# Attention and two feed-forward layers on one core: split tiles written through ACT's queue, three raw buffers, whole weight tiles, a held attention chain with work on POOL

## The chip, the cores and the metric

One core of a Trainium2 chip runs the whole program. TensorE (PE) has 128 rows and columns; VectorE (DVE), ScalarE (ACT) and GpSimd (POOL) work on its results, and SyncE (SP) issues DMAs. The metric is device time in microseconds of one execution.

## The reference

The first layer is a linear attention over 8 batches of 8 heads, 576 positions and 64 columns; its output, 4608 tokens by 512, goes through a squared-ReLU feed-forward layer of width 2048, then through RMS normalisation and a gated layer of width 1536. All is float32; the weights come as float64.

```python
q_s = exp(q - max(q, -1));  q_s = q_s / (sum(q_s, -1) + 1e-09)
k_s = exp(k - max(k, 2));   k_s = k_s / (sum(k_s, 2) + 1e-09)
kv = einsum('bhsd,bhse->bhde', k_s, v)
x = einsum('bhsd,bhde->bhse', q_s, kv)        # then as 4608 x 512
r = maximum(x @ moe_w_in, 0.0);  x = (r * r) @ moe_w_out
xn = x / sqrt(mean(x * x, -1) + 1e-06) * rms_g
g = xn @ w_gate
out = (g * (1 / (1 + exp(-g))) * (xn @ w_val)) @ w_out
```

## The kernel before

The 4608 tokens are nine blocks of 512. Stage 1 does attention and the first feed-forward layer of all blocks, stage 2 the gated layer, with a Strassen-like scheme of seven products of halves (STEPS).

Every operand of PE is split into two reduced-precision parts, the rounded value (ACT, L73) and the remainder (DVE, L74), and each product is three passes of PE over those parts (mm3, L92).

A unit of stage 1 is one 128-column slice c of the 2048 columns for one block j: p1_A (L526) does 12 matmuls into ps_h, ReLU, square and split; p1_B (L538), two units later, 12 matmuls into the accumulators. There are 16 units a block and 144 in all. In between, each unit runs what is due at it: weight preparation (tick, L308) and attention of the next block (todo, L763).

Weight preparation takes a tile of 128 by 512 float64 words through four stages, one stage a tick: d_load (DMA into one of two raw buffers, by SP), d_words (POOL takes the high words, L211, and ACT the low ones, L219), d_float (three operations on DVE, L230 to L242) and d_split (the rounded copy on ACT, L246, and the remainder on POOL, L247). In block 0 the 32 tiles of the first layer are made, about two a unit, and used at once from a ring of seven; all but eight, which stay, are also written to DRAM, by a DMA on SP's queue right after the split (L253). In blocks 1 to 6 the tiles of the gated layer follow, with sums and differences of quarters on POOL (L278), and are written through two buffers so (L261 to L263), again by SP. Later blocks load split tiles from DRAM into the ring (feed, L159); SP waits at each load for the slot's last reader.

Attention works in pairs of heads, hp = 0 to 3, four for each block. A_STEPS (L760) gives each step's unit beside the pair's start, A_STARTS, every three units: k and q are loaded three units ahead (a_load), v one ahead, then come the maxima and the q-subtraction with its exponential (a_q), a unit later the normalisation of q (a_qn, L455) and the spreading of k's column maxima (a_ktr, with PE for blocks 0 and 1 and DVE transposes after), then q's transposes on PE (a_qT), the k-subtraction (L427) and exponential (a_kexp), a unit later the product of k and v and its normalisation into block-diagonal tiles kvd (a_kv, with L493 and L494), and a unit later the product with q (a_x) into ps_x and its split x, which is the operand of the next block's p1_A. q, k and v tiles have two buffers each.

The program is traced in this order, and a scheduler then orders each engine's instructions by its own cost model and tells each what to wait for; on the chip each engine runs its list in order. `tc.keep_in_program_order(ins)` pins an instruction behind everything already traced on its engine.

Of the kernel before, what the change touches and what calls it, by code (L numbers as in the profile page):

```python
# [24 lines left out]
def attention_moe_kernel(  # L25
# [7 lines left out]
    w_gate: bass.AP,  # L33
    w_val: bass.AP,
# [4 lines left out]
    nc = tc.nc  # L39
# [8 lines left out]
    FF1 = w_in.shape[1] // P  # L48
    FF2 = w_gate.shape[1] // P
# [19 lines left out]
    ]  # L69
    x2d = [tc.dram_tile([P, KD, T], F32, name=f"x2d{j}") for j in range(NB)]  # L70
# [31 lines left out]
    NTAG = 8  # L102
# [81 lines left out]

    raws, words, floats = {}, {}, {}

    def halves(n, c, r):
        rows = slice(r * (DM // 2), (r + 1) * (DM // 2))
        cols = slice((2 * n + c) * P, (2 * n + c + 1) * P)
        return [w[rows, cols].rearrange("(k p) f -> p k f", p=P) for w in (w_gate, w_val)]  # L190

    def d_load(key):
        n, c = key
        r = pools["d"].tile([P, 512], U64, tag="raw", name="raw", bufs=2)
        if n == "i":
            src = w_in[:, c * P : (c + 1) * P].rearrange("(k p) f -> p k f", p=P)
            nc.sync.dma_start(out=r.rearrange("p (k f) -> p k f", k=KD), in_=src)
        elif n in ("o", "u"):
            w = w_out if n == "o" else w_out2
            nc.sync.dma_start(out=r, in_=w[c * P : (c + 1) * P, :])  # L200
        else:
            for g, src in enumerate(halves(c, int(n[0]) - 1, int(n[1]) - 1)):
                rv = r.rearrange("p (g k f) -> p g k f", g=2, k=2)
                nc.sync.dma_start(out=rv[:, g], in_=src)
        raws[key] = r
# [102 lines left out]
    def tick():  # L308
        n = ticks[0]
        for stage, ahead in ((d_split, 0), (d_float, 1), (d_words, 2), (d_load, 3)):  # L310
            if 0 <= n - 3 + ahead < len(jobs):
                key = jobs[n - 3 + ahead]
                if key is None:
                    continue
                if stage == d_split and n - 3 + ahead >= NJ1:
                    stage = d_quad
                stage(key)
        ticks[0] += 1

# [4 lines left out]
    kts, kes, vts, qts, qns, mks, mcs, qTs = {}, {}, {}, {}, {}, {}, {}, {}  # L324
# [9 lines left out]
    def a_load(j, hp):  # L334
        hs = slice(2 * hp, 2 * hp + 2)
        if j < B:
            kt = a_tile(j, hp, [2, SF + 1, D], "kt")
            nc.gpsimd.memset(kt[SR:P, :, SF, :], -3e38)
            nc.sync.dma_start(
                out=kt[:, :, 0:SF, :],  # L340
                in_=k[j, hs, 0 : SF * P, :].rearrange("h (p c) d -> p h c d", c=SF),
            )
            nc.sync.dma_start(
                out=kt[0:SR, :, SF, :], in_=k[j, hs, SF * P : S, :].rearrange("h p d -> p h d")
            )
            kts[j, hp] = kt
        qt = a_tile(j, hp, [2, NG, D], "qt")
# [38 lines left out]
    def a_ktr(j, hp):  # L386
        if j >= B:
            return
        if j > 1:
# [3 lines left out]
            mb = pools["a"].tile([P, P], F32, tag="mb", name="mb", bufs=1)  # L393
# [19 lines left out]
        mb = pools["a"].tile([P, P], F32, tag="mb", name="mb", bufs=1)  # L413
# [3 lines left out]
    def a_kexp(j, hp):  # L417
# [7 lines left out]
        kt = kts.pop((j, hp))  # L425
        mx = ps[:, 0:P].rearrange("p (h d) -> p h d", h=2).unsqueeze(2)
        nc.vector.tensor_tensor(  # L427
            out=kt, in0=kt, in1=mx.to_broadcast([P, 2, SF + 1, D]), op=ALU.subtract
        )
        ke = pools["a"].tile([P, SF + 1, 2, D], F32, tag="ke", name="ke", bufs=1)  # L430
        nc.scalar.activation(out=ke, in_=kt.rearrange("p h c d -> p c h d"), func=AF.Exp)
        kes[j, hp] = ke

    def a_q(j, hp):
        qt = qts[j, hp]
        qv = qt.rearrange("p h c d -> p (h c) d")
        n = 2 * NG
        qm = pools["a"].tile([P, n], F32, tag="qm", name="qm")
        nc.vector.reduce_max(out=qm, in_=qv, axis=AX.X)
        (nc.gpsimd if j == 0 else nc.vector).tensor_tensor(  # L440
            out=qv, in0=qv, in1=qm.unsqueeze(2).to_broadcast([P, n, D]), op=ALU.subtract
        )
        nc.scalar.activation(out=qv, in_=qv, func=AF.Exp)

    def a_qn(j, hp):
        qt = qts.pop((j, hp))
        qv = qt.rearrange("p h c d -> p (h c) d")
        n = 2 * NG
        qs = pools["a"].tile([P, n], F32, tag="qs", name="qs")
        nc.vector.reduce_sum(out=qs, in_=qv, axis=AX.X)  # L450
        nc.vector.tensor_scalar_add(out=qs, in0=qs, scalar1=1e-9)
        nc.vector.reciprocal(out=qs, in_=qs)
        qn = pools["a"].tile([P, NG, 2, D], F32, tag="qn", name="qn", bufs=2)
        rs = qs.rearrange("p (h c) -> p h c", h=2).unsqueeze(3)
        nc.vector.tensor_tensor(  # L455
# [16 lines left out]
    def a_kv(j, hp):
# [4 lines left out]
        for c in range(SF + 1):  # L477
            m = P if c < SF else SR
            for h in range(2):
                nc.tensor.matmul(  # L480
# [5 lines left out]
                )  # L486
        rk = pools["a"].tile([P, 1], F32, tag="rk", name="rk")
        nc.vector.tensor_scalar_add(out=rk, in0=ps[:, D : D + 1], scalar1=1e-9)
        nc.vector.reciprocal(out=rk, in_=rk)
        t = kvd[j % 2][hp]  # L490
        for h in range(2):
            r = slice(h * D, (h + 1) * D)
            nc.vector.tensor_scalar_mul(out=t[r, 0, r], in0=ps[r, 0:D], scalar1=rk[r])  # L493
            nc.vector.scalar_tensor_tensor(  # L494
                out=t[r, 1, r],
                in0=ps[r, 0:D],
                scalar=rk[r],
                in1=t[r, 0, r].bitcast(F32),
                op0=ALU.mult,
                op1=ALU.subtract,  # L500
            )

    def a_x(j, hp):
# [5 lines left out]
        for b, lo, hi in ((j - 1, 0, p0), (j, p0, P)):  # L509
            if lo == hi:  # L510
# [266 lines left out]
    with ExitStack() as ctx_a:  # L777
# [5 lines left out]
        for hp in range(NP):  # L783
            a_load(0, hp)
# [6 lines left out]
        for row in kvd:  # L791
            for t in row:
                nc.gpsimd.memset(t.bitcast(F32), 0.0)
# [3 lines left out]
            "m": a_kmax, "q": a_q, "n": a_qn, "r": a_ktr, "e": a_kexp, "t": a_qT, "v": a_kv, "x": a_x  # L797
        }
        for step in (
# [5 lines left out]
            else:  # L805
                first[step[0]](0, int(step[1]))
# [6 lines left out]
        for i, (j, c) in enumerate(units):  # L813
# [60 lines left out]


# [27 lines left out]
```

## Time and profile before

| | |
|---|---|
| Median of 3 runs | 1823.58 us (1822.58 to 1827.39) |
| Profiled execution | 1824.28 us, its span 1822.5 us |
| PE, PEld busy | 1750.0 us (96%), 1516.4 us (83%) |
| DVE, ACT, POOL busy | 1163.1 us (64%), 744.9 us (41%), 227.3 us (12%) |
| DMA | 423.35 MB, mean 232 GB/s |

The page cuts the span into 40 slices of 45.6 us; a digit is the busy share in tenths:

```profile
PE   5888989999999999999999999999999999999998
...
DVE  8987987768687654321336666675767676757544
ACT  3654545555545434333443333423233333333322
POOL 4553224333414100000000000000000000000000
```

The first 21 digits are stage 1. POOL's work ends with weight preparation, in the 14th. A share averages over stages: what an engine costs is read where others wait for it.

### The profile page before, as it was taken

What the parts mean: (1) busy time and instruction counts of PE and PEld (TensorE: products, weight loads), DVE (VectorE), ACT (ScalarE), POOL (GpSimd) and SP (SyncE); (2) the same over time, 40 slices, a digit from 0 to 9 for tenths busy, and PEclk for the clock granted to TensorE, in tenths of its full rate; (3) what the DMA queues carried; (4) which work ended last, traced back from release to release, by engine and by line L of the source; (5) the groups of instructions that cost most, each with busy time, mean ns of one, the idle gap of its engine ahead of it and who ended that gap; (6) DMA issues with size and microseconds to landing.
All of it is one profiled execution on the core that took longest, in us unless ns stands there. A gap on an engine that the chain in (4) does not pass through costs nothing.

```text
span 1822.5 us, 27487 instructions
## 1 busy us (share of the span) xinstructions
PE 1750.0 (96%) x10298; PEld 1516.4 (83%) x10298; DVE 1163.1 (64%) x2080; ACT 744.9 (41%) x1279; POOL 227.3 (12%) x265
## 2 busy tenths in 40 slices
PE   5888989999999999999999999999999999999998
PEld 3666878778877888888888989898999999999997
DVE  8987987768687654321336666675767676757544
ACT  3654545555545434333443333423233333333322
POOL 4553224333414100000000000000000000000000
PEclk9998999999999999999999999999999999999999
DMA  6778878898878855445767666767676767676673
GB/s 191 228 235 267 269 249 290 268 298 268 299 259 286 267 177 172 160 140 208 256 214 233 221 246 215 242 222 255 209 257 213 255 209 261 212 244 217 214 237 131
DMA packets 190244, 423.35 MB, mean 232 GB/s; under 512 B 57888, under 2 KB 95776, under 8 KB 188960
## 3 DMA queue, kind: packets, MB, share of 16 engines
q1 hardware_dynamic: 190112, 421.60, 69.6%
q8 instruction: 82, 1.34, 0.3%
q14 instruction: 50, 0.41, 0.1%
HBM read 361.76 MB, written 59.77 MB: 231 GB/s over the span
## 4 chain that ended last, share of the span: by engine, by line
PE 76%; DVE 10%; DMA 6%; issue 2%; ACT 2%; SPq 2%; POOL 1%; DVEq 0%; POOLq 0%; ACTq 0%
PE acc L94 31%; PE ps_h L94 15%; PE ps_x L668 8%; PE ps_y L668 8%; PE ps_v L668 8%; PE ps_w L668 4%; DMA kt<-in_k_dram 2%; DMA out_dram<-e 2%; DVE t L242 1%; DVE t L238 1%; PE ps_x L94 1%; DVE g L74 1%; DVE t L230 1%; PE ps_kv L480 1%; DVE mk L381 1%
## 5 line engine op out<-in xcount | busy, mean ns | idle before, releaser
L94 PE MATMUL ps_h<-x,ws 128*128 128x512 f32 x1296 | 328.3, 402 | 5.7 <-POOL ws L247 4.7
L94 PE MATMUL acc<-g,ws 128*128 128x512 f32 x1296 | 315.5, 392 | 7.8 <-ACT ws L246 3.4
L74 DVE TENSOR_TENSOR g<-r,g 128x512 fp32r<-128x512 f32 x252 | 186.9, 742 | 172.6 <-ACT g L73 169.9
L94 PEld LDWEIGHTS acc<-g,ws 128*128 128x128 f32 x1296 | 243.3, 188 | 62.2 <-ACT ws L246 4.2
L94 PEld LDWEIGHTS ps_h<-x,ws 128*128 128x128 f32 x1296 | 242.8, 192 | 59.2 <-POOL ws L247 7.0
L94 PE MATMUL acc<-ws,g 128*128 128x512 f32 x1080 | 267.1, 392 | 0.0
L94 PEld LDWEIGHTS acc<-ws,g 128*128 128x128 f32 x1080 | 195.5, 189 | 36.4
L73 ACT ACTIVATE g<-r 128x512 fp32r<-128x512 f32 x252 | 157.9, 627 | 35.1 <-DVE r L652 30.8
L650 ACT ACTIVATE sg<-c 128x256 f32<-128x256 f32 x108 | 56.5, 523 | 262.8 <-DVE c L683 213.3
L532 ACT ACTIVATE r<-ps_h 128x512 f32<-128x512 f32 x144 | 85.3, 593 | 190.6 <-PE ps_h L94 190.0
L683 DVE TENSOR_TENSOR u<-ps_y,p 128x512 f32<-128x512 f32 x108 | 73.9, 684 | 124.2 <-PE ps_y L668 124.2
L668 PE MATMUL ps_x<-x,ws 128*128 128x256 f32 x972 | 130.5, 284 | 10.1 <-ACT p L699 10.1
L668 PEld LDWEIGHTS ps_x<-x,ws 128*128 128x128 f32 x972 | 122.1, 191 | 11.8 <-ACT p L699 11.7
L668 PEld LDWEIGHTS ps_v<-x,ws 128*128 128x128 f32 x864 | 114.1, 191 | 6.4
L668 PE MATMUL ps_v<-x,ws 128*128 128x256 f32 x864 | 116.0, 282 | 0.0
L94 PE MATMUL ps_h<-x,w 128*128 128x512 f32 x432 | 109.2, 399 | 2.5 <-DVE x L74 1.9
L94 PE MATMUL acc<-g,w 128*128 128x512 f32 x432 | 105.7, 393 | 3.9 <-DVE g L74 1.9
L706 ACT ACTIVATE p<-ps_v 128x512 f32<-128x512 f32 x54 | 32.3, 599 | 174.8 <-PE ps_v L668 174.8
L683 DVE TENSOR_TENSOR c<-ps_v,u 128x512 f32<-128x512 f32 x54 | 37.4, 692 | 100.0 <-PE ps_v L668 99.7
L668 PE MATMUL ps_y<-x,ws 128*128 128x256 f32 x756 | 100.9, 283 | 0.0
L94 PEld LDWEIGHTS acc<-g,w 128*128 128x128 f32 x432 | 81.4, 189 | 21.9 <-DVE g L74 2.3
L94 PEld LDWEIGHTS ps_h<-x,w 128*128 128x128 f32 x432 | 80.6, 190 | 21.8 <-DVE x L74 2.5
(118 smaller groups left out, 2521.0 us busy)
## 6 DMA issues: line engine op xcount, KB each, us to landing
ws<-wd_s SPq DMA_DIRECT2D x135, 512.0 KB, 4.3
ws<-wd_a SPq DMA_DIRECT2D x117, 512.0 KB, 4.5
ws<-wd_i SPq DMA_DIRECT2D x96, 512.0 KB, 4.6
ws<-wd_o SPq DMA_DIRECT2D x96, 512.0 KB, 4.5
ws<-wd_u SPq DMA_DIRECT2D x90, 512.0 KB, 4.1
raw<-in_moe_w_out_dram SPq DMA_DIRECT2D x28, 512.0 KB, 5.3
wd_s<-so SPq DMA_DIRECT2D x24, 512.0 KB, 5.8
x2d<-e SPq DMA_DIRECT2D x36, 256.0 KB, 3.2
```

The lines of the kernel that those rows point to most:

```text
L73: nc.scalar.activation(out=dst[:, 0], in_=src, func=AF.Copy)
L74: nc.vector.tensor_tensor(out=dst[:, 1], in0=src, in1=dst[:, 0].bitcast(F32), op=ALU.subtract)
L94: nc.tensor.matmul(ps, lhsT(a), rhs(b), start=first and n == 0, stop=last and n == 2)
L230: nc.vector.tensor_scalar(out=t, in0=sb, scalar1=3, scalar2=0x7FFFFFFF, op0=ALU.logical_shift_left, op1=ALU.bitwise_and,)
L238: nc.vector.scalar_tensor_tensor(out=t, in0=sb, scalar=0x80000000, in1=t, op0=ALU.bitwise_and, op1=ALU.bitwise_or)
L242: nc.vector.tensor_tensor(out=ti, in0=ti, in1=n, op=ALU.add)
L381: nc.vector.tensor_reduce(out=mk, in_=kts[j, hp].rearrange("p h c d -> p h d c"), axis=AX.X, op=ALU.max)
L532: nc.scalar.activation(out=r, in_=ps, func=AF.Relu)
L650: nc.scalar.activation(out=r, in_=h[:, :, 0], func=AF.Sigmoid)
L668: nc.tensor.matmul(ps[:, g * HF : (g + 1) * HF], w[:, wa, (2 * g + kk) * P : (2 * g + kk + 1) * P], x[:, xa, kk, :], start=first and g == ...
L683: nc.vector.tensor_tensor(out=sv(name), in0=in0, in1=in1, op=ALU.add)
L706: nc.scalar.activation(out=sv("p5"), in_=ps, func=AF.Copy)
```

## The change

Eight edits, all of them in stage 1 or in the layout of the inputs:

- Written tiles are put on a list (send) and their DMAs issued later (flush) by ACT, pinned in ACT's order: tiles of the ring after two more ticks, tiles `so` at the flush of the unit after. `so` gets three buffers.
- raw gets three buffers, and d_load runs four ticks ahead of the split in place of three; the tick counts in n_ticks are one higher.
- The host lays out each weight tile as one contiguous block, so that d_load is one DMA for every kind of tile, and w_gate and w_val are one input. The values stay float64.
- The steps of attention are split (a_loadk, a_loadq, a_qmax, a_qsub, a_qexp, a_qsum, a_qn, a_ksub, a_kexp, a_kv, a_kvd) and spread over units -2 to 7 of a pair in place of -3 to 4; pairs start at units -2, 1, 4, 7.
- From block 1 on (`held`, j > 0) the pinned instructions are the q-subtraction, both exponentials, q's sum, the scaling, the k-subtraction, the first transpose of a_qT, the first matmul of a_kv, the first of each product of a_x, and the ACT half of the splits.
- The q-subtraction, the scaling of q (for all blocks) and the k-subtraction (from block 2 on) run on POOL.
- kvd is made from one DVE operation, the product with 1/sum and with a constant mask of two blocks, and a split (ACT, DVE) over all 128 columns, in place of two operations on each half; the eight zero fills of kvd go. qt gets three buffers and mb two.
- NTAG goes from 8 to 9 (one more weight tile stays in SBUF), the tile sg moves to another pool, and the DMA scratch of the program is set to 1024.

```diff
-    def split(dst, src):
-        nc.scalar.activation(out=dst[:, 0], in_=src, func=AF.Copy)
+    def held(j, ins):
+        return tc.keep_in_program_order(ins) if j > 0 else ins
+
+    def split(dst, src, j=0):
+        held(j, nc.scalar.activation(out=dst[:, 0], in_=src, func=AF.Copy))
...
-    NTAG = 8
+    NTAG = 9
...
-        r = pools["d"].tile([P, 512], U64, tag="raw", name="raw", bufs=2)
...
+        r = pools["d"].tile([P, 512], U64, tag="raw", name="raw", bufs=3)
+        if n in ("i", "o", "u"):
+            src = {"i": w_in, "o": w_out, "u": w_out2}[n][c]
         else:
-            for g, src in enumerate(halves(c, int(n[0]) - 1, int(n[1]) - 1)):
...
+            src = w_gv[int(n[1]) - 1, int(n[0]) - 1, c]
+        nc.sync.dma_start(out=r, in_=src)
...
+    late = []
+
+    def send(key, t, after):
+        late.append([after, key, t])
+
+    def flush(all=False):
+        for x in late:
+            x[0] -= 1
+        while late and (late[0][0] < 0 or all):
+            _, key, t = late.pop(0)
+            tc.keep_in_program_order(nc.scalar.dma_start(out=wd[key], in_=flat(t)))
...
         if key not in res1:
-            nc.sync.dma_start(out=wd[key], in_=flat(t))
+            send(key, t, 2)
...
-            t = pools["q"].tile([P, 2, 512], F32R, tag="so", name="so", bufs=2)
+            t = pools["q"].tile([P, 2, 512], F32R, tag="so", name="so", bufs=3)
             w_split(t, f(), nc.gpsimd)
-            nc.sync.dma_start(out=wd[key], in_=flat(t))
+            send(key, t, 1)
...
-        for stage, ahead in ((d_split, 0), (d_float, 1), (d_words, 2), (d_load, 3)):
+        for stage, ahead in ((d_split, 0), (d_float, 1), (d_words, 2), (d_load, 4)):
...
+        if n < NJ1 + 4:
+            flush()
...
+        ins = (nc.gpsimd if j > 1 else nc.vector).tensor_tensor(
+            out=kt, in0=kt, in1=mx.to_broadcast([P, 2, SF + 1, D]), op=ALU.subtract
+        )
+        held(j, ins)
...
+        held(j, nc.gpsimd.tensor_tensor(out=qv, in0=qv, in1=qm, op=ALU.subtract))
...
-        nc.vector.tensor_tensor(
+        ins = nc.gpsimd.tensor_tensor(
             out=qn.rearrange("p c h d -> p h c d"),
...
-        for h in range(2):
-            r = slice(h * D, (h + 1) * D)
-            nc.vector.tensor_scalar_mul(out=t[r, 0, r], in0=ps[r, 0:D], scalar1=rk[r])
-            nc.vector.scalar_tensor_tensor(
...
+        f = pools["a"].tile([P, P], F32, tag="kvf", name="kvf")
+        nc.vector.scalar_tensor_tensor(
+            out=f.rearrange("p (h d) -> p h d", h=2),
+            in0=ps[:, 0:D].unsqueeze(1).to_broadcast([P, 2, D]),
+            scalar=rk,
+            in1=mask,
+            op0=ALU.mult,
+            op1=ALU.mult,
+        )
+        split(kvd[j % 2][hp], f, j)
...
-    A_STEPS = ((-3, a_load), (-1, a_loadv), (0, a_q), (0, a_kmax), (1, a_qn), (1, a_ktr), (2, a_qT))
-    A_STEPS += ((2, a_kexp), (3, a_kv), (4, a_x))
-    A_STARTS = (0, 3, 6, 9)
+    A_STEPS = ((-2, a_loadk), (-2, a_loadq), (0, a_qmax), (0, a_kmax), (1, a_qsub), (1, a_ktr))
+    A_STEPS += ((1, a_loadv), (2, a_ksub), (2, a_qexp), (3, a_kexp), (3, a_qsum), (4, a_kv))
+    A_STEPS += ((4, a_qn), (5, a_kvd), (5, a_qT), (7, a_x))
+    A_STARTS = (-2, 1, 4, 7)
...
+            if ticks[0] > NJ1 + 4:
+                flush()
```

## Rows read from the trace of the kernel before

**Rows 1.** Timeline of ACT, first ReLU of block 0: start, us, instruction, idle

```profile
49.00 1.09 ACT L532 ACTIVATE r<-ps_h 128x512 f32<-128x512 f32 x2 [2.22 <-PE ps_h L94]
```

**Rows 2.** From:to, us; PE, PEld, DVE, ACT, POOL busy (count), clock, DMA

```profile
0.00:49.00 49.00, 27.11 (x140) 17.68 (x141) 41.01 (x83) 18.57 (x30) 24.39 (x46) 1.00 0.67 191
49.00:172.60 123.60, 105.04 (x480) 79.02 (x479) 102.54 (x168) 68.37 (x119) 58.97 (x60) 0.93 0.75 244
172.60:275.90 103.30, 98.54 (x504) 80.47 (x503) 93.12 (x195) 51.05 (x87) 23.75 (x29) 0.98 0.82 259
275.90:377.10 101.20, 99.67 (x515) 81.26 (x514) 76.98 (x147) 52.76 (x89) 37.66 (x38) 1.00 0.85 279
377.10:474.60 97.50, 95.14 (x497) 77.19 (x496) 74.80 (x145) 52.08 (x89) 30.65 (x34) 1.00 0.90 293
474.60:582.80 108.20, 102.86 (x518) 83.31 (x517) 76.47 (x143) 52.43 (x89) 37.09 (x39) 0.98 0.80 273
582.80:679.00 96.20, 94.30 (x492) 77.24 (x491) 63.02 (x125) 45.34 (x77) 14.40 (x18) 1.00 0.72 237
679.00:776.30 97.30, 97.30 (x505) 79.88 (x504) 38.60 (x85) 40.10 (x66) 0.43 (x3) 1.00 0.50 161
...
955.40:1822.50 867.10, 850.89 (x5852) 791.90 (x5851) 546.27 (x922) 288.73 (x518) 0.00 (x0) 1.00 0.68 226
```

**Rows 3.** Waits in block 0: engine and line, releaser: us, times, longest

```profile
DVE t L230 <- POOL s L211: 11.8, 5, 3.9
...
ACT n L219 <- DMA raw<-in_moe_w_out_dram: 5.7, 4, 4.1
...
POOL s L211 <- DMA raw<-in_moe_w_in_dram: 4.8, 4, 1.8
```

**Rows 4.** DVE groups in block 0: shapes, count, busy us, mean ns, idle

```profile
L238 DVE SCALAR_TENSOR_TENSOR t<-s,t 128x512 uint32<-128x512 uint32 x27 | 25.6, 949 | 0.5
...
L440 DVE TENSOR_TENSOR qt<-qt,qm 128x512 f32<-128x512 f32 x4 | 4.4, 1089 | 0.1
...
L455 DVE TENSOR_TENSOR qn<-qt,qs 128x512 f32<-128x512 f32 x4 | 3.2, 791 | 0.0
...
L493 DVE TENSOR_SCALAR kvd<-ps_kv,rk 64x64 fp32r<-64x64 f32 x8 | 2.2, 281 | 0.2
```

**Rows 5.** Waits of SP's queue in block 0

```profile
SPq L253 <- POOL ws L247: 58.3, 19, 5.3
```

**Rows 6.** Waits of SP's queue in blocks 1 to 5

```profile
SPq L350 <- DVE qn L455: 53.9, 12, 7.8
SPq L263 <- POOL so L247: 37.8, 17, 6.0
```

**Rows 7.** Chain of waits in block 4: start us, us, what

```profile
536.39 0.33 SPq L350
...
543.27 5.74 DMA kt<-in_k_dram
...
549.13 1.36 DVE mk L381
...
557.92 0.70 DVE qn L455
...
558.63 0.33 SPq L350
```

**Rows 8.** Waits of all engines from 172 to 583 us (blocks 1 to 4)

```profile
POOL so L247 <- ACT so L246: 107.0, 32, 11.3
...
PE ps_x L94 <- DVE kvd L493: 7.8, 5, 4.7
```

**Rows 9.** Group on DVE in block 6, the q-subtraction

```profile
L440 DVE TENSOR_TENSOR qt<-qt,qm 128x512 f32<-128x512 f32 x4 | 2.8, 692 | 0.1
```

**Rows 10.** Group on POOL in the start (0 to 49 us), the q-subtraction

```profile
L440 POOL TENSOR_TENSOR qt<-qt,qm 128x512 f32<-128x512 f32 x4 | 4.1, 1042 | 6.4 <-DVE qm L439 6.4
```

**Rows 11.** Part 5 of the page: ACT's copy of a split

```profile
L73 ACT ACTIVATE g<-r 128x512 fp32r<-128x512 f32 x252 | 157.9, 627 | 35.1 <-DVE r L652 30.8
```

More of the change, by code (lines that the diff above doesn't have):

```diff
@@ L47, in attention_moe_kernel @@
     NP = H // 2
-    FF1 = w_in.shape[1] // P
-    FF2 = w_gate.shape[1] // P
+    FF1 = w_in.shape[0]
+    FF2 = w_out2.shape[0]
     SF = S // P
@@ L430, in a_kexp, with q_heads @@
         ke = pools["a"].tile([P, SF + 1, 2, D], F32, tag="ke", name="ke", bufs=1)
-        nc.scalar.activation(out=ke, in_=kt.rearrange("p h c d -> p c h d"), func=AF.Exp)
+        ins = nc.scalar.activation(out=ke, in_=kt.rearrange("p h c d -> p c h d"), func=AF.Exp)
+        held(j, ins)
         kes[j, hp] = ke
[L434 to L443, printed above, removed]
+    def q_heads(j, hp):
+        return qts[j, hp].rearrange("p h c d -> p (h c) d")
@@ new lines, in a_qmax, with a_qsub, a_qexp @@
+    def a_qmax(j, hp):
+        qm = pools["a"].tile([P, 2 * NG], F32, tag="qm", name="qm")
+        nc.vector.reduce_max(out=qm, in_=q_heads(j, hp), axis=AX.X)
+        qms[j, hp] = qm
+    def a_qsub(j, hp):
+        qv = q_heads(j, hp)
+        qm = qms.pop((j, hp)).unsqueeze(2).to_broadcast([P, 2 * NG, D])
+        held(j, nc.gpsimd.tensor_tensor(out=qv, in0=qv, in1=qm, op=ALU.subtract))
+    def a_qexp(j, hp):
+        qv = q_heads(j, hp)
+        held(j, nc.scalar.activation(out=qv, in_=qv, func=AF.Exp))
@@ L445, in a_qn, with a_qsum @@
+    def a_qsum(j, hp):
+        qs = pools["a"].tile([P, 2 * NG], F32, tag="qs", name="qs")
+        held(j, nc.vector.reduce_sum(out=qs, in_=q_heads(j, hp), axis=AX.X))
+        nc.vector.tensor_scalar_add(out=qs, in0=qs, scalar1=1e-9)
+        nc.vector.reciprocal(out=qs, in_=qs)
+        qms[j, hp] = qs
     def a_qn(j, hp):
         qt = qts.pop((j, hp))
[L447 to L450, printed above, removed]
@@ L460, in a_qn @@
         )
+        held(j, ins)
         qns[j, hp] = qn
@@ L486, in a_kv, with a_kvd @@
                 )
+                if c == 0 and h == 0:
+                    held(j, ins)
+        kvs[j, hp] = ps
+    def a_kvd(j, hp):
+        if j >= B:
+            return
+        ps = kvs.pop((j, hp))
         rk = pools["a"].tile([P, 1], F32, tag="rk", name="rk")
@@ L790, in attention_moe_kernel @@
         nc.gpsimd.memset(eps_sb, 1e-6)
-        for row in kvd:
-            for t in row:
-                nc.gpsimd.memset(t.bitcast(F32), 0.0)
+        for h in range(2):
+            for g in range(2):
+                nc.gpsimd.memset(mask[h * D : (h + 1) * D, g, :], 1.0 if g == h else 0.0)
         nc.sync.dma_start(out=g_sb, in_=rms_g.rearrange("(m p) -> p m", p=P))
         first = {
-            "m": a_kmax, "q": a_q, "n": a_qn, "r": a_ktr, "e": a_kexp, "t": a_qT, "v": a_kv, "x": a_x
+            "m": (a_kmax,),
+            "q": (a_qmax, a_qsub, a_qexp),
+            "n": (a_qsum, a_qn),
+            "r": (a_ktr,),
+            "e": (a_ksub, a_kexp),
+            "t": (a_qT,),
+            "v": (a_kv, a_kvd),
+            "x": (a_x,),
         }
@@ L805, in attention_moe_kernel @@
             else:
-                first[step[0]](0, int(step[1]))
+                for f in first[step[0]]:
+                    f(0, int(step[1]))
         for i in sorted(todo):
@@ L829, in attention_moe_kernel @@
             if i == n1 - FF1 - 1:
-                assert not outs and ticks[0] == len(jobs) + 3
+                assert not outs and ticks[0] == len(jobs) + 4
+                flush(all=True)
                 ctx_q.close()
@@ L895, with tiles @@
-    for i, (shape, dtype) in enumerate(_OUTS):
-        dt = _mybir.dt.from_np(_np.dtype(dtype))
-        args.append(nc.dram_tensor(f"out_{i}_dram", shape, dt, kind="ExternalOutput").ap())
+    P = 128
+    def tiles(name, dims, order, shape):
+        t = _np.ascontiguousarray(inputs[name]).view(_np.uint64).reshape(dims).transpose(order)
+        return _np.ascontiguousarray(t).reshape(shape)
+    a = {name: _np.ascontiguousarray(inputs[name]) for name in ("q", "k", "v")}
+    d, ff = inputs["moe_w_in"].shape
@@ new lines @@
+    a["w_in"] = tiles("moe_w_in", (d // P, P, ff // P, P), (2, 1, 0, 3), (ff // P, P, d))
+    a["w_out"] = tiles("moe_w_out", (ff // P, P, d), (0, 1, 2), (ff // P, P, d))
+    d, ff = inputs["moe2_w_gate"].shape
+    dims = (2, d // P // 2, P, ff // P // 2, 2, P)
+    t = [
+        tiles(name, dims, (0, 4, 3, 2, 1, 5), (2, 2, ff // P // 2, P, d // 2))
+        for name in ("moe2_w_gate", "moe2_w_val")
+    ]
+    a["w_gv"] = _np.concatenate(t, axis=-1)
+    a["w_out2"] = tiles("moe2_w_out", (ff // P, P, d), (0, 1, 2), (ff // P, P, d))
@@ new lines @@
+    a["rms_g"] = inputs["moe2_rms_g"]
+    nc = _bacc.Bacc(
+        "TRN2", target_bir_lowering=False, num_devices=1, dynamic_dma_scratch_size=1024
+    )
+    arrays, args = {}, []
+    for name in a:
+        arrays[f"in_{name}"] = _np.ascontiguousarray(a[name])
+        dt = _mybir.dt.from_np(arrays[f"in_{name}"].dtype)
+        shape = arrays[f"in_{name}"].shape
+        args.append(nc.dram_tensor(f"in_{name}", shape, dt, kind="ExternalInput").ap())
+    b, h, s, e = a["q"].shape
+    out = nc.dram_tensor("out", (b * s, h * e), _mybir.dt.float32, kind="ExternalOutput")
```

144 lines of the change are left out of this document (57 added, 87 removed).

## The prediction

> **What bounds the kernel now.** I first cut the span into the nine token blocks of stage 1, at every sixteenth ReLU of L532 (the first is at 49.00 us), and asked for the busy time of every engine in each piece [rows 1, 2]. Stage 2, from 955.4 us on, has PE busy 850.9 of 867.1 us, and nothing in it depends on attention or on weight preparation. Block 6 (679.0 to 776.3) has a full block's attention, no weight work, and PE busy for all of its 97.3 us: that is the price of a block when nothing is late. Against it block 0 takes 123.6, block 1 103.3, block 2 101.2, block 3 97.5, block 4 108.2, block 5 96.2 us, and 49.0 us go by before the first ReLU. So 47 us at most lie in blocks 0 to 4, the start apart, and there the change works.
>
> Second, the waits and the groups of block 0. DVE is busy 102.5 of 123.6 us [rows 2]. It idles 11.8 us behind POOL's unpacking of raw weights, and POOL and ACT in their turn wait for raw tiles to land [rows 3]. DVE also runs its operations slower than elsewhere: the mask-and-or of L238 takes 949 ns [rows 4].
>
> Third, SP's own waits. SP is one queue in order. In block 0 it stands 58.3 us at the write of a split tile (L253), waiting for POOL to finish it; in blocks 1 to 5 it stands 53.9 us at the load of q (L350), waiting for the normalisation of the pair two before, which frees one of two q buffers, and 37.8 us at L263 [rows 5, 6]. Behind it queue ring loads, raw loads and k.
>
> Fourth, the chain of waits in block 4. It closes on itself: the q load is let go by the normalisation (L455), k lands behind it, then come the maximum of k and the chain to the next normalisation, which lets the next q load go [rows 7]. From one q load to the next are 558.63 - 536.39 = 22.2 us, where a pair is due every three units, 3 x 97.3 / 16 = 18.2 us. This makes attention late, and PE pays at a_x, where it waits for kvd in lumps of up to 4.7 us [rows 8].
>
> **The change part by part.**
>
> *q-subtraction and scaling to POOL, kvd rewritten.* In block 0 DVE loses 4 x 1.09 us (L440), 4 x 0.79 us (L455) and 16 small kvd operations of 0.28 us (L493, and L494 like it), 4.4 + 3.2 + 4.5 = 12.1 us [rows 4]. It gets for each pair one masked product and one subtraction over 128 columns; nearest are those 64-column ones, 0.28 us, and 0.69 us for 512 columns [rows 9]; I take 0.29, 2.3 us in all (bounds 2.2 and 5.5). POOL gets eight operations. POOL's own subtraction of this shape took 1.04 us in the start and DVE's in block 6 0.69 us [rows 9, 10], so 8.3 us; with DVE beside it, more, and I take 10. More POOL work slows DVE: L238 at 949 against the 690 or so of its size undisturbed (the 692 of a like-sized operation) is 27 x 0.26 = 7 us for 59.0 us of POOL [rows 2, 4, 9]. Taking all of DVE's weight work as twice that, 0.24 us for one of POOL, 10 us cost 2.4 (bounds 0 and 10). DVE's work in block 0 becomes 102.5 - 12.1 + 2.3 + 2.4 = 95.1 us. From block 1 on POOL also gets the k-subtraction, 640 columns, 1.04 x 640 / 512 = 1.3 us at the least: 4 x (2 x 1.04 + 1.3) = 13.5 us a block beside the 23.8 to 37.7 that it has [rows 2]. [...]
>
> *Raw tiles: three buffers, four ticks ahead, one contiguous load.* A raw tile now has two ticks to land where it had one. In block 0 that takes away waits of 5.7 us on ACT and about as much on POOL (4.8 for w_in, and one more row like it for w_out) [rows 3], and with them most of DVE's 11.8 us behind POOL. Bounds for DVE: 0 to 11.8 us; I take 7.5, since some of that POOL time is POOL waiting for ACT, which stays. One DMA in place of two for gate and value halves SP's issues there; I count that at nothing, since PE never waited for it.
>
> *Writes late and through ACT.* SP's 58.3 and 37.8 us of standing go. They aren't on PE's path by themselves: what they gave is lateness of the raw loads and of k, counted above and below. What is late next on SP is the ring load, which waits for PE and may. ACT gets an issue for each write, 0.33 us by SP's rows [rows 7]: 23 in block 0, 7.6 us, where ACT is idle for 55 of 123.6 us [rows 2]. Each is traced one unit or two ticks behind its tile, so POOL should be done with it; if not, ReLU, square and split of the units stand behind it on ACT, and PE two units later. [...]
>
> *The kvd split on ACT* is one more activation per pair. By the 627 ns of a 512-column one [rows 11], four are between 0 and 2.5 us a block, in ACT's idle time.
>
> *Held chain, three q buffers, more distance.* From a_kv to a_x there were one unit, now three; kvd's result has two units before PE needs it. The loop of block 4 is cut: with three buffers a q load waits for the pair three before. Block 0 then has DVE's 95.1 us and the idle time that stays, 123.6 - 102.5 - 7.5 = 13.6: 108.7, say 109 (bounds: 99, PE's price with this block's extra transposes, to 120). Block 1 loses the lump of 4.7: 99. Block 2: 98.5. Block 3 stays 97.5. Block 4 comes down to 98.5 (bounds 97.3 and 108.2). Block 5 is 1.1 us under block 6 because block 4 pushed work about; I take 97.
>
> *Start.* DVE loses four normalisations and the kvd work, about 3.2 + 2.2 us of its 41.0, POOL gets at least 4.2 of it and the first pair of block 1 is begun before the first unit. Bounds -5 and +5, taken as 0. One more resident tile takes a ring load out of each of blocks 1 to 8 and of the nine blocks of stage 2, 17 in all; no ring load held PE, so 0.
>
> Sum: 14.6 + 4.3 + 2.7 + 0 + 9.7 - 0.8 = 30.5 us. The profiled execution took 1824.28 us around its span of 1822.5, so 1793.8; the median of the runs is 0.7 lower, so 1793.
>
> **The rivals.**
>
> *A, block 0 keeps its time.* DVE's relief is eaten: POOL's 10 us stop DVE for 10, which leaves 12.1 - 2.3 - 10 = -0.2 us of it, and the waits for raw tiles turn into waits of POOL for ACT. For it: DVE's 949 ns; against it: over block 0 DVE's slowing was a quarter of POOL's time, not all of it. Blocks 1, 2, 4 and 5 still give 15.9: 1793 + 14.6 = 1808.
>
> *B, the loop only changes its link.* k still has two buffers and now five units from load to exponential, as before; then k paces the pairs and blocks 1 to 4 keep their time. For it: the k load is the longest piece of the loop [rows 7]; against it: SP no longer stands in front of it. Block 0 alone gives 14.6: 1793 + 15.9 = 1809.
>
> *C, slower: POOL becomes the link.* The k-subtraction is held behind all that POOL has, and POOL stood up to 11.3 us behind ACT's copy [rows 8]. From subtraction to exponential is one unit, 97.3 / 16 = 6.1; what is beyond it, 11.3 - 6.1 = 5.2 us, reaches PE at a held a_kv, and a lower granted clock after it (0.98 in block 4 [rows 2]) comes on top. The gain is gone from 30.5 / 5.2 = 6 pairs on; if half of the 20 pairs of blocks 1 to 5 meet it, 1793 + 52 = 1845. Against it: with raw tiles early and three output tiles, POOL's longest waits should shrink.
>
> *D, nothing.* The pinned order puts other waits in the place of each one removed; within 0.3% (5.5 us, what a measurement of this kernel can tell from no change) of 1823.
>
> **How the numbers follow.** Forecast 1793, its own range 1779 to 1806 (block 0 at 99 with the start 4 better; or block 0 at 116 and blocks 1 to 4 each 1.5 worse): 0.62. A 0.16, B 0.09, C 0.07, D 0.06. Faster has the first three, 0.87; same 0.06; slower 0.07. The range 1777 to 1816 takes in A and B and leaves out D, C and the forecast's tails, some 2 in 10.
>
> **What would show it.** Right: SP without waits on POOL or on the normalisation; blocks 1 to 5 within 2 us of 97.3; block 0 near 109 with DVE at about 95 us; no PE wait for kvd of over 1 us; granted clock 1.00 from block 1 on; stage 2 at 867. Wrong: POOL waits on PE's path at a_kv or a_qT (C), k loads still let go by ACT's exponential with 20 us between pairs (B), block 0 over 118 (A), or a start over 52 us.

## The result and the profile after

Median 1848.11 us (1846.58 to 1852.94) against 1825.19 for the kernel before on the same chip: ratio 1.0131, 95% interval [1.0105, 1.0157]. The change makes the kernel 1.3% slower; the forecast was 1793, in a range of 1777 to 1816. The profiled execution took 1846.61 us around a span of 1844.8. The ratios of the experiments below leave out two executions far off the rest, one of f4_spwrites at 7118 us and one of i1_best at 6049.

The first ReLU now starts at 40.22 us (49.00 in [rows 1]). From the first ReLU of each block the span was cut as in [rows 2]. The view of windows of the kernel after (columns as there):

```profile
0.00:40.20 40.20, 22.10 (x133) 15.12 (x133) 30.55 (x63) 17.12 (x30) 23.28 (x43) 0.87 0.70 197
40.20:175.20 135.00, 107.04 (x489) 77.03 (x488) 115.66 (x186) 69.20 (x127) 86.97 (x78) 0.96 0.77 256
175.20:280.50 105.30, 97.67 (x503) 80.23 (x502) 72.86 (x135) 51.10 (x90) 46.35 (x44) 0.97 0.72 235
280.50:389.30 108.80, 99.30 (x505) 81.36 (x504) 57.71 (x106) 47.87 (x84) 37.69 (x37) 0.95 0.68 222
389.30:497.10 107.80, 99.53 (x506) 81.43 (x505) 64.67 (x126) 48.62 (x85) 43.59 (x41) 0.95 0.71 230
497.10:605.60 108.50, 100.64 (x507) 82.16 (x506) 63.00 (x116) 50.29 (x88) 39.48 (x38) 0.97 0.70 229
605.60:705.80 100.20, 98.22 (x504) 81.00 (x503) 62.72 (x120) 49.55 (x87) 46.38 (x43) 0.98 0.73 236
981.90:1844.80 862.90, 854.05 (x5852) 793.72 (x5850) 545.41 (x922) 289.53 (x518) 0.00 (x0) 1.00 0.68 222
```

Read together with [rows 2]: the start is 8.8 us shorter and block 0 11.4 longer, so their sum went from 172.6 to 175.2 and not to 158. Blocks 1 to 5 take 530.6 us where they took 506.4, with a granted clock of 0.95 to 0.98. Stage 2 is 4.2 us shorter.

The waits from 175 to 706 us, the five blocks that lost (engine, line, releaser: us, times, longest):

```profile
POOL so L244 <- ACT so L243: 88.7, 19, 25.1
POOL qn L487 <- DVE qs L480: 86.9, 13, 33.2
...
POOL kt L445 <- DVE mb L424: 68.9, 15, 15.0
```

SP's own queue in the same stretch no longer waits where [rows 6] had it wait for POOL at a write. The q load (now L368) stands longer than before, 83.1 us in place of 53.9, behind POOL's normalisation:

```profile
SPq L368 <- POOL qn L487: 83.1, 13, 11.0
```

Where PE pays is seen in its waits from 172 to 600 us; before, the longest was 4.7 us [rows 8]:

```profile
PE ps_q L501 <- DVE rk L535: 21.4, 4, 7.6
PE ps_q L501 <- DVE kvf L539: 8.4, 1, 8.4
```

One of them, from the timeline of the kernel after (start us, us, engine, instruction, idle before it and its releaser):

```profile
212.15 0.58 ACT L77 ACTIVATE x<-ps_x 128x512 fp32r<-128x512 f32 x1
...
213.38 1.25 DVE L424 STREAM_TRANSPOSE mb<-mk 32x128 f32<-32x128 f32 x4
...
214.71 2.03 POOL L445 TENSOR_TENSOR kt<-kt,mb 128x640 f32<-128x640 f32 x1 [3.17 <-DVE mb L424]
216.71 0.63 POOL L208 TENSOR_SCALAR s<-raw 128x512 f32<-128x512 f32 x1
...
217.38 1.30 DVE L227 TENSOR_SCALAR t<-s 128x512 uint32<-128x512 uint32 x1 [2.03 <-POOL s L208]
...
220.16 0.68 DVE L78 TENSOR_TENSOR x<-ps_x,x 128x512 fp32r<-128x512 f32 x1
220.76 0.15 DVE L535 TENSOR_SCALAR rk<-ps_kv 128x1 f32<-128x1 f32 x1
...
220.98 1.09 PE L501 MATMUL ps_q<-ident,qn 128*128 128x128 f32 x4 [7.63 <-DVE rk L535]
```

POOL stood 3.17 us for DVE's maximum with the weight work (L208) behind the k-subtraction; DVE then stood 2.03 us for that weight work, and behind it the remainder of x (L78), whose first half ACT had done at 212.73, and L535. PE's transposes of the next pair (L501) start only after these reads of PSUM. Two engines, each in its own order, wait for each other in turn here, 3.17 and 2.03 us, and PE stands 7.63 us.

The clock adds to it. Windows of the kernel after around a like stall in block 2 (columns as in the first fence):

```profile
310.00:318.80 8.80, 8.80 (x58) 7.26 (x57) 5.93 (x11) 2.88 (x6) 5.96 (x5) 1.00 0.29 112
318.80:327.60 8.80, 0.44 (x2) 0.02 (x2) 8.10 (x12) 2.33 (x4) 5.95 (x7) 0.72 1.00 306
327.60:333.00 5.40, 5.37 (x15) 4.43 (x16) 5.20 (x8) 4.13 (x9) 2.48 (x3) 0.50 1.02 344
333.00:338.00 5.00, 5.00 (x23) 4.10 (x23) 3.24 (x6) 3.52 (x6) 0.96 (x1) 1.00 0.67 192
```

PE did nearly nothing for 8.8 us, with a granted clock of 0.72 in the mean; the clock then stood at 0.50 for the next 5.4 us, though PE was busy for 5.37 of them, and at 1.00 after that. Twelve matmuls into ps_h that started at 328.36 took 5.13 us; twelve like them at 306.31, with the clock at 1.00, took 2.88. If 5.4 us at 0.50 do the work of 2.7 at 1.00, the stall cost about 11.5 us by this estimate, not 8.8.

### The profile page after: what moved, and what is told of

Read it like the earlier page. It is cut to its first block, busy times and chain, and to the rows that moved or that the text cites. A ratio compares the mean times of both kernels' runs of the same rounds, so it can differ in the third digit from the quotient of the medians.

```text
span 1844.8 us, 27327 instructions
## 1 busy us (share of the span) xinstructions
PE 1754.7 (95%) x10298; PEld 1520.9 (82%) x10298; DVE 1101.0 (60%) x1924; ACT 745.9 (40%) x1311; POOL 356.3 (19%) x353
## 4 chain that ended last, share of the span: by engine, by line
PE 76%; DVE 5%; DMA 4%; POOL 3%; issue 2%; ACT 1%; SPq 0%; ACTq 0%; POOLq 0%; DVEq 0%
PE acc L98 30%; PE ps_h L98 15%; PE ps_x L715 8%; PE ps_v L715 8%; PE ps_y L715 8%; PE ps_w L715 4%; DMA wd_a<-so 1%; DMA wd_s<-so 1%; POOL so L244 1%; DVE t L227 1%; PE ps_x L98 1%; DVE t L235 1%; POOL kt L445 1%; DVE t L239 1%; PE ps_q L501 1%
## 5 line engine op out<-in xcount | busy, mean ns | idle before, releaser
L78 DVE TENSOR_TENSOR g<-r,g 128x512 fp32r<-128x512 f32 x252 | 188.3, 747 | 228.9 <-ACT g L77 226.4
L98 PE MATMUL ps_h<-x,ws 128*128 128x512 f32 x1188 | 306.4, 407 | 8.7 <-POOL ws L244 6.9
L98 PEld LDWEIGHTS ps_h<-x,ws 128*128 128x128 f32 x1188 | 228.1, 196 | 59.2 <-POOL ws L244 9.3
L98 PE MATMUL acc<-ws,g 128*128 128x512 f32 x972 | 244.2, 395 | 2.9 <-ACT g L77 2.9
L98 PEld LDWEIGHTS acc<-ws,g 128*128 128x128 f32 x972 | 176.1, 190 | 36.8 <-ACT g L77 4.3
L98 PE MATMUL ps_h<-x,w 128*128 128x512 f32 x540 | 134.4, 396 | 1.7 <-POOL w L244 1.1
L98 PEld LDWEIGHTS ps_h<-x,w 128*128 128x128 f32 x540 | 100.0, 189 | 24.6 <-POOL w L244 1.5
```

The lines of the kernel that those rows point to most:

```text
L78: nc.vector.tensor_tensor(out=dst[:, 1], in0=src, in1=dst[:, 0].bitcast(F32), op=ALU.subtract)
L98: ins = nc.tensor.matmul(ps, lhsT(a), rhs(b), start=first and n == 0, stop=last and n == 2)
```

## The experiments

A ratio is to the kernel before on the same chip, with its 95% interval; differences between runs are of their medians. The theories: **W**, the weight side costs (W1 its late writes through ACT, W2 the raw tiles earlier); **P**, POOL's attention operations cost; **H**, the pinned order costs.

**The weight side alone** (e3_wonly): attention of before, preparation of after.

```diff
-            nc.sync.dma_start(out=wd[key], in_=flat(t))
+            send(key, t, 2)
...
-        r = pools["d"].tile([P, 512], U64, tag="raw", name="raw", bufs=2)
+        r = pools["d"].tile([P, 512], U64, tag="raw", name="raw", bufs=3)
...
-            t = pools["q"].tile([P, 2, 512], F32R, tag="so", name="so", bufs=2)
+            t = pools["q"].tile([P, 2, 512], F32R, tag="so", name="so", bufs=3)
```

> The kernel before with the weight side of the change alone: late writes through ACT, three raw and three output buffers, four ticks ahead, whole tiles, nine resident tiles; attention as it was. P and H: faster than before, 1800 to 1818, since SP no longer stands for POOL and raw tiles are early. W: 1840 or more.

1838.47 us, 1.0084 [1.0069, 1.0100], just under W's range: none of the attention edits is needed for a loss. ACT's side of it, in the timeline of this kernel (ACTq is the issue of a DMA in ACT's list):

```profile
207.21 1.74 POOL L243 TENSOR_TENSOR so<-t,so 128x512 fp32r<-128x512 f32 x1
...
208.99 0.33 ACTq L255 DMA_DIRECT2D wd_a<-so  x1
209.36 0.60 ACT L542 ACTIVATE r<-ps_h 128x512 f32<-128x512 f32 x1 [4.18 <-POOL so L243]
...
215.71 0.63 ACT L242 ACTIVATE so<-s 128x512 fp32r<-128x512 f32 x1 [4.42 <-DMA wd_a<-so]
...
216.80 0.58 ACT L76 ACTIVATE qT<-ps_q 128x512 fp32r<-128x512 f32 x1
...
217.41 0.69 DVE L77 TENSOR_TENSOR qT<-ps_q,qT 128x512 fp32r<-128x512 f32 x1 [3.72 <-ACT qT L76]
```

The write waits for POOL's split, and the ReLU waits behind it on ACT for 4.18 us. Then ACT's next split wants an output tile that this same write has yet to empty: 4.42 us more. The split of qT stands behind that, DVE's half of it behind ACT's, and kvd behind that on DVE, at 224.96; PE reaches its products with kvd at 226.38, after 6.69 us of waiting.

**After without the new weight timing** (e4_oldw): writes at once by SP with two output tiles, two raw buffers, three ticks; the rest of after stays.

```diff
-            send(key, t, 2)
+            nc.sync.dma_start(out=wd[key], in_=flat(t))
...
-        r = pools["d"].tile([P, 512], U64, tag="raw", name="raw", bufs=3)
+        r = pools["d"].tile([P, 512], U64, tag="raw", name="raw", bufs=2)
...
-        for stage, ahead in ((d_split, 0), (d_float, 1), (d_words, 2), (d_load, 4)):
+        for stage, ahead in ((d_split, 0), (d_float, 1), (d_words, 2), (d_load, 3)):
```

> The changed kernel with writes issued by SP right after the split, two raw and two output buffers and three ticks ahead; whole tiles, nine resident tiles and the new attention stay. P and H: 1840 to 1870, as slow as the changed kernel or slower. W: 1825 or less.

1816.28 us, 0.9956 [0.9939, 0.9973]: 32 us under after, and now faster than before.

**After with the attention operations back on DVE** (e1_dve), and **without pins in attention** (e2_nohold).

```diff
-        ins = (nc.gpsimd if j > 1 else nc.vector).tensor_tensor(
+        ins = nc.vector.tensor_tensor(
...
-        held(j, nc.gpsimd.tensor_tensor(out=qv, in0=qv, in1=qm, op=ALU.subtract))
+        held(j, (nc.gpsimd if j == 0 else nc.vector).tensor_tensor(out=qv, in0=qv, in1=qm, op=ALU.subtract))
...
-        ins = nc.gpsimd.tensor_tensor(
+        ins = nc.vector.tensor_tensor(
```

> The changed kernel with the q-subtraction of blocks 1 to 8, the scaling of q and the k-subtraction on DVE, all else as it is, pins too. Theory P (POOL's three attention operations are the link: POOL stands for DVE with the unpacking of raw tiles behind it, DVE's weight work and the split of x then stand behind POOL, the PSUM slot of x stays taken and PE waits at the transposes of q): no PE wait of over 2 us at the transposes in blocks 1 to 5, blocks 1 to 5 at 98 to 101 us, time 1805 to 1822. Theory H (the pinned order and the new spacing are the link, on whichever engine): lumps of 5 us and more stay, time 1840 or more. Theory W (the writes on ACT's queue): 1840 or more.

1836.61 us, 1.0069 [1.0054, 1.0084].

```diff
-        return tc.keep_in_program_order(ins) if j > 0 else ins
+        return ins
```

> The changed kernel with no pins in attention (the write DMAs stay pinned on ACT), POOL work as in the changed kernel. P: the lumps stay in some form, 1835 to 1855. H: lumps gone, 1800 to 1820. W: 1840 or more.

1837.76 us, 1.0081 [1.0066, 1.0096]. Each gives back 10 to 12 us of 23: P and H fall as the main cause, and stay as parts. The first time lies in none of the ranges that were set for it.

**W taken apart**, each on the weight side alone. Raw tiles early, but writes at once by SP, with two output tiles (f1_rawonly):

```diff
-            send(key, t, 2)
+            nc.sync.dma_start(out=wd[key], in_=flat(t))
```

Writes late by ACT, but raw tiles as before (f2_actwrites), by the raw lines of e4's diff. Writes late, pinned, but on SP (f4_spwrites), and writes by ACT, unpinned (g3_actfree):

```diff
-            tc.keep_in_program_order(nc.scalar.dma_start(out=wd[key], in_=flat(t)))
+            tc.keep_in_program_order(nc.sync.dma_start(out=wd[key], in_=flat(t)))
```

```diff
-            tc.keep_in_program_order(nc.scalar.dma_start(out=wd[key], in_=flat(t)))
+            nc.scalar.dma_start(out=wd[key], in_=flat(t))
```

> e3_wonly with the writes back on SP right after the split and two output buffers; three raw buffers and four ticks ahead stay. Theory W1 (the late writes on ACT's queue are what costs: ACT stands for POOL at the issue and then for the landing of a write that left late): stage 1 back to before's, time 1812 to 1822 with what stage 2 gives. Theory W2 (the earlier raw loads cost: on SP they stand for ACT to free a buffer, with q, k and the ring loads behind): 1832 or more.

> e3_wonly with two raw buffers and three ticks ahead; late writes through ACT with three output buffers stay. W1: 1832 to 1845. W2: 1812 to 1822.

> e3_wonly with the late writes pinned on SP's queue in place of ACT's, at the same place in the order and with the same buffers. W1, if it is ACT's standing that costs: 1815 to 1825. If it is the lateness of the write, whichever queue issues it (the output buffer comes back later and ACT's copy waits for it): 1830 or more. W2: 1832 or more.

> e3_wonly (weight side alone) with the write DMAs on ACT but not pinned, so that the scheduler places them by its own model. If the pin and the order that it makes on ACT cost: 1815 to 1822. If an issue on ACT's queue costs wherever it stands, since ACT waits there for POOL's split and its units behind it: 1830 or more.

f1 1815.01 us, 0.9955 [0.9934, 0.9976]; f2 1831.49, 1.0041 [1.0026, 1.0056]; f4 1818.2, 0.9961 [0.9946, 0.9976]; g3 1842.61, 1.0108 [1.0085, 1.0130]. W2 falls as the main cause, but not altogether: the early raw tiles make f2 into e3 and, in the new attention, e4 into g2 (below), and cost about 7 us each time (1831.49 to 1838.47, 1816.28 to 1823.03). The one word from scalar to sync is worth 20.3 us (e3 to f4), lateness and pins unchanged; it is ACT's queue that costs, pinned or not. PE's longest waits from 172 to 600 us, of e3:

```profile
PE ps_x L97 <- DVE kvd L503: 20.8, 6, 6.7
```

and of f4, with f1 at 5.8 us:

```profile
PE ps_x L97 <- DVE kvd L503: 7.5, 6, 3.0
```

The granted clock of this stretch is 0.97 in e3 and 1.00 in f4. ACT's waits for a landed write go the same way: 54.7 us in e3 (22.4 + 21.0 + 11.3), 22.9 in f4 (9.7 + 9.4 + 3.8). Its waits for POOL right behind an issue, like the 4.18 us above, are few: 8.5 us in all of stage 1 of e3. So most of what ACT's queue adds is the second wait of the timeline, for an output tile whose write left late. Such waits are not by themselves the measure: f1, with two output tiles, has 57.0 us of them (25.4 + 20.4 + 11.2). What differs is what stands behind them: in the timeline above it is the split of qT. That this is so in every case is argued from it, not shown.

Whole weight tiles and the DMA scratch size were not tried alone.

**The gate's scratch tile in the other pool** (f3_sg), the part of the weight side that frees room for the ninth tile, alone on before.

```diff
-        r = gp.tile([P, n, HF], F32, tag="sg", name="sg", bufs=2)
+        r = pools["x"].tile([P, n, HF], F32, tag="sg", name="sg", bufs=2)
```

> The kernel before with the tile sg moved to the other pool alone. All kernels of the change so far run stage 2 by 4 to 8 us faster, always in the first two groups of a block. If the move of sg is that gain: 1815 to 1820, stage 1 as before. If it is the ninth resident tile or another edit: 1823, no change.

1824.38 us, 0.9998 [0.9987, 1.0009]: nothing.

**The same on the whole change**: after with its late writes on SP (g1_splate), after with writes at once by SP (g2_spnow), and g2 with POOL's three attention operations on DVE (g4_spnow_dve). The diffs are those of f4, f1 and e1.

> The changed kernel with the late writes pinned on SP's queue in place of ACT's, all else as it is. If ACT's queue is the main cause (f4 against e3: 20 us): 1822 to 1832, with what POOL's attention operations cost left. If POOL's operations are the main cause and ACT's queue only adds where attention is old: 1840 or more.

> The changed kernel with the writes on SP right after the split and two output buffers, so e4_oldw with three raw buffers and four ticks. ACT's queue as main cause: 1808 to 1822. The other: 1835 or more.

> g2_spnow with the attention operations of POOL back on DVE (as in e1_dve). If POOL's operations cost by themselves (e1_dve was 11 us under the changed kernel): 5 to 12 us under g2_spnow. If they only cost beside ACT's queue: the same as g2_spnow within 3 us, or slower since DVE has more to do.

g1 1831.59 us, 1.0044 [1.0029, 1.0058]; g2 1823.03, 0.9998 [0.9983, 1.0014]; g4 1809.47, 0.9922 [0.9902, 0.9942]. ACT's queue costs 16.5 us here too (after to g1), the late writes with their third output tile 8.6 more (g1 to g2), and POOL's operations 13.6 (g2 to g4); g2 and g4 lie 1 to 2 us outside what was expected of them.

**Which of POOL's operations** (h1_kdve): g2 with the k-subtraction alone on DVE.

> The kernel after with each write at once on SP's queue (1823.0 us), and of POOL's three attention operations only the k-subtraction put back on DVE; q-subtraction and normalisation stay on POOL. With all three back it was 1809.5. Theory K (the k-subtraction, 1.9 us on POOL, costs, because it stands between DVE's maximum and ACT's exponential, and DVE's and PE's next steps stand behind it): most of the 13.6 us comes back, 1810 to 1814. Rival Q (the normalisation on POOL costs, because the q loads wait for it): little comes back, 1819 to 1823. If the price is POOL's load as such, by busy time, about half: 1815 to 1818.

1805.49 us, 0.9903 [0.9886, 0.9920], 17.5 under g2 and below the range of theory K: all of the cost is the k-subtraction's, and the two q operations may stay on POOL. Windows of this kernel, blocks 1 to 5:

```profile
174.30:271.20 96.90, 96.90 (x506) 79.75 (x505) 79.07 (x155) 51.78 (x89) 39.34 (x43) 1.00 0.87 275
271.20:373.90 102.70, 100.40 (x513) 81.98 (x513) 71.18 (x125) 54.67 (x95) 46.83 (x46) 0.98 0.88 294
373.90:471.10 97.20, 96.16 (x503) 79.11 (x503) 64.88 (x126) 52.17 (x92) 43.94 (x46) 1.00 0.89 287
471.10:571.60 100.50, 97.17 (x505) 79.51 (x504) 71.27 (x135) 53.16 (x96) 43.49 (x43) 1.00 0.83 283
571.60:667.10 95.50, 95.50 (x500) 79.15 (x499) 42.84 (x95) 41.45 (x73) 14.71 (x19) 1.00 0.60 195
```

PE's wait for L535 from 172 to 600 us, in g2 and in h1:

```profile
PE ps_q L501 <- DVE rk L535: 12.2, 5, 4.2
```

```profile
PE ps_q L501 <- DVE rk L535: 3.0, 3, 1.7
```

It is down to a quarter. The q load's wait for POOL's normalisation in h1 is 13.9 us from 175 to 580 us.

**Without pins again** (h2_nohold: g4, i1_best: h1) **and the ninth resident tile** (h4_ntag8: g4 with eight; i2_ntag9: f3 with nine). The diffs are that of e2, and NTAG.

> The fastest kernel so far (writes at once on SP, all attention operations on DVE, 1809.5 us) without the pins of the attention chain. If the pins hold other work up in this state too, as they did in the kernel after (10.4 us in medians), 1800 to 1805. If they cost there only because POOL and ACT's queue were late behind them, within 3 us of 1809.5. If they are worth what they are for, slower: 1813 to 1820.

> The kernel after with writes at once on SP, the k-subtraction on DVE, and no pins in attention; q-subtraction and normalisation stay on POOL. If the gains of the last two steps add (1809.5 to 1805.5 for the two q operations on POOL, 1809.5 to 1804.4 without pins), 1800 to 1801. If both cure the same lateness, 1804 to 1806.

> The same fastest kernel (1809.5 us) with eight resident weight tiles in place of nine. Every kernel with nine spends 1.3 us less from one token block to the next in stage 2 (94.4 against 95.7), about 8 us over the stage. Theory: the ninth tile is the cause, stage 2 goes back to about 95.7 a block and the time to 1815 to 1819. Rival: the whole, contiguous weight tiles or the split writes' order are the cause, stage 2 stays at 94.4 a block and the time within 3 us of 1809.5.

> The kernel before with the ninth resident weight tile alone (and the gate's scratch tile in the other pool, which alone moved nothing: 1824.4). By the step of the prediction that counted the ninth tile at nothing: 1821 to 1826. By the run with eight tiles in place of nine (11 us more): 1812 to 1816, with stage 2 at 94.4 us a block in place of 95.7.

h2 1804.44 us, 0.9887 [0.9864, 0.9911], 5 under g4; i1 1811.8, 0.9929 [0.9913, 0.9946], 5 to 6 over h1 and in neither of its ranges. In both pairs the intervals overlap, so these runs give the pins no sign of their own. h4 1820.73, 0.9985 [0.9971, 0.9999]: the ninth tile is worth 11 us there. i2 1829.58, 1.0039 [1.0025, 1.0054]: on the kernel before it costs 6, and lies in neither of its ranges. Between token blocks of stage 2, by the first matmul of each, lie 94.3 us in i2 and 95.7 in before. There the ninth tile acts alike in both pairs: a wait of PE in stage 2 of before,

```profile
PE ps_x L668 <- ACT p L699: 10.1, 8, 2.0
```

has its like in h4 (9.5 us) and none in i2 and g4. The loss of i2 is then in stage 1. What costs there was not tried.

h1 and h2 beat both kernels, the one before by 1.0 and 1.1%; their intervals overlap.

## Why the prediction was wrong

**The step that failed first is the writes through ACT.** It was costed at nothing: 7.6 us of issues in ACT's idle time, with POOL done by then. It measures 16.5 us in the whole change (g1) and 20.3 in the weight side alone (f4). The prediction named the condition ("if not, ReLU, square and split of the units stand behind it on ACT") and gave it no price. Idle time of ACT was the wrong cover: an issue costs ACT not its 0.33 us alone but the wait for what it sends (4.18 us in the timeline of e3) and, more often here, for an output tile that a late write has yet to empty (4.42 us there), and behind ACT stands the split of qT, not only the units. In neither pair of runs did ACT's queue give a gain over SP's. Writing late was counted as harmless too, and cost 8.6 us with the new attention (g1 to g2); with the old it is within the intervals (f1 and f4).

**The k-subtraction on POOL was mis-sized and misplaced.** The estimate was 1.3 us at the least. The group on POOL from 175 to 706 us:

```profile
L445 POOL TENSOR_TENSOR kt<-kt,mb 128x640 f32<-128x640 f32 x23 | 43.2, 1879 | 69.2 <-DVE mb L424 68.9
```

It is 1.88 us, and the larger price, as the timeline above has it, is the 68.9 us that POOL stands in front of it while weight work queues behind. The sum held its busy time against POOL's share, where the place in POOL's order decides. Putting it back gives 17.5 us (g2 to h1).

**Block 0's 14.6 us never came.** Start and block 0 together took 172.6 us before; in no kernel here did they take under 170.0 (f4), and in h1 174.3. DVE's work did not shrink: 41.0 + 102.5 before, 30.55 + 115.66 after, 2.7 more where 7.4 less was forecast for block 0 alone. What was to leave DVE did leave it: the q-subtractions, normalisations and kvd operations took 19.3 us in start and block 0, the new kvd operations take 8.9. But the earlier pair starts bring about 10 us of block 2's attention into the same stretch, which the prediction had nowhere; before, none of its maxima were spread there. In the groups on DVE in block 0 of the kernel after:

```profile
L424 DVE STREAM_TRANSPOSE mb<-mk 32x128 f32<-32x128 f32 x8 | 2.4, 301 | 0.2
```

DVE's work in block 1 fell from 93.12 to 72.86 us, this being part of it. A smaller term is the remainder of kvd, in block 0 and in block 6, where POOL is busy for only 22.73 of 97.2 us, two rows of the groups on DVE:

```profile
L78 DVE TENSOR_TENSOR kvd<-kvf,kvd 128x128 fp32r<-128x128 f32 x4 | 4.5, 1124 | 0.0
```

```profile
L78 DVE TENSOR_TENSOR kvd<-kvf,kvd 128x128 fp32r<-128x128 f32 x4 | 1.1, 281 | 0.0
```

0.29 was right where POOL is out of its way, and 1.12 where it is not; with the masked product (1.4) kvd took 5.9 us of block 0, over the bound of 5.5. The 7.5 us of DVE's idle time for the raw tiles failed otherwise: in f1 DVE's wait behind POOL's unpacking is 3.5 us in place of 11.8 [rows 3], but start and block 0 are only 1.8 shorter, and DVE's wait for ACT's copy of g rose from 1.6 to 6.1; over the whole kernel the early raw tiles cost about 7 us (e4 to g2). What stays is the turn-taking itself, in the waits of block 0 of f1:

```profile
POOL ws L243 <- ACT ws L242: 29.1, 17, 3.6
ACT ws L242 <- DVE t L238: 13.8, 12, 2.2
...
ACT w L242 <- DVE t L238: 11.9, 6, 3.5
```

Before, the three were 36.5, 13.6 and 6.7: 56.8 in all, now 54.8. A weight tile goes DVE, ACT, POOL in series; DVE's share of block 0 was read as the bound, and was not the only one. That the turn-taking holds block 0 is argued from these rows; no run shows it.

**The loop of block 4 was cut only where POOL is free.** After: 108.5 us for 98.5 forecast, since the link from normalisation to q load moved from DVE to POOL, which stands in front of k. In h1, with three q buffers and the same steps, blocks 1, 3, 4 and 5 take 96.9, 97.2, 100.5 and 95.5 for 99, 97.5, 98.5 and 97: there the step holds within 2.1 us. Only block 2, 102.7 for 98.5, stays over. The forecast of 1793 for the whole is missed even by the best kernels by 11 to 13 us, less than block 0's term alone.

**Start and stage 2.** The start was taken as 0 within 5 and is 8.8 us shorter, with block 0 longer by more; DVE's normalisations and kvd operations there were put at 3.2 and 2.2 us and were 2.7 and 4.4. The ninth tile, counted at nothing because no ring load held PE, changes 11 us with one sign and 6 with the other. The term left out is PE's wait for ACT's copy in stage 2, 10.1 us in before and gone with nine tiles, so the change reaches stage 2 too; what the tile does to stage 1 stays open.

**Of the rivals**, A rested on POOL's 10 us in block 0 stopping DVE for 10, which no run tried alone; what the runs show is the remainder of kvd, with 4.5 us beside POOL's work in block 0 for 1.1 in block 6. C came nearest: POOL as the link, 1845 us, a chance of 0.07. Its place was not the one it named: PE waits at the transposes of q, for DVE, not at a held a_kv, and five stalls of 3 to 9 us with the clock behind them make it, not ten of 5.2, so that its number comes within 3 us is luck. And it is one cause of two; the other, ACT's queue, no rival had. Its condition against ("POOL's longest waits should shrink") is refuted: 25.1 us at the longest where it was 11.3 [rows 8].

## What to carry to other kernels

A DMA issue placed on a compute engine's queue (here 16.5 and 20.3 us) is to be costed by what that engine then waits for, the tile it sends and the buffer that its write frees late, with everything behind it, and not by its own length against idle time. The same holds for an operation moved to an engine with idle time: ask what it waits for when its turn comes and what stands behind it there. The resident tile gave a gain on one version of this pipeline and a loss on another, and the early raw tiles, forecast as a gain, cost 7 us on two: measure such an edit on the version that is kept.

## What the runs showed of the hardware that was not expected

An operation of DVE with both inputs in SBUF waited out the subtraction that POOL was running, four times of four (0.31 to 1.40 us for 0.28), and one with an input in PSUM did not (0.69 us, as usual). In block 0 of the kernel after, with POOL busy 86.97 of 135 us, the remainder of kvd, whose two inputs both lie in SBUF, takes 1124 ns in the mean for 281 in block 6. The mean is made of 1.39, 1.40, 0.31 and 1.40 us. The first and the third, each with the POOL operation beside it and the third with DVE's operation before, which reads PSUM:

```profile
76.71 1.27 POOL L244 TENSOR_TENSOR w<-t,w 128x512 fp32r<-128x512 f32 x1
76.74 1.39 DVE L78 TENSOR_TENSOR kvd<-kvf,kvd 128x128 fp32r<-128x128 f32 x1
```

```profile
131.98 1.71 POOL L244 TENSOR_TENSOR ws<-t,ws 128x512 fp32r<-128x512 f32 x1
...
132.92 0.69 DVE L78 TENSOR_TENSOR qT<-ps_q,qT 128x512 fp32r<-128x512 f32 x1
...
133.53 0.31 DVE L78 TENSOR_TENSOR kvd<-kvf,kvd 128x128 fp32r<-128x128 f32 x1
```

All four end 0.15 us after the POOL subtraction that was under way when they began; the remainder of qT takes its usual 0.69 us in the midst of one. In block 6 POOL is idle beside three of the four, and beside the fourth it begins 0.01 us after DVE. So the price in these four is what was left of POOL's operation, and the mean of 1124 ns tells little of it. The masked product, with one tensor in PSUM and one in SBUF, takes 347 ns in block 0 for 350:

```profile
L539 DVE SCALAR_TENSOR_TENSOR kvf<-ps_kv,rk,mask 128x128 f32<-128x128 f32 x4 | 1.4, 347 | 0.1
```

That the old kvd, 281 ns in before's block 0, where POOL is busy 58.97 of 123.6 us [rows 2, 4], was cheap because it read PSUM, and that the rewrite gave this up, fits these two groups; it was not tried.
